# The first tile's two halves on two queues: sync engine and ScalarE, with the first two weights changed over

## The chip, the core and the metric

The kernel runs on one core of a Trainium2 chip. A core has TensorE (PE, matrix products), VectorE (DVE), ScalarE (ACT), GpSimd (POOL) and SyncE (SP). Transfers between the large memory (HBM) and the on-chip memory (SBUF) are put on queues by SP, ACT or GpSimd and moved by 16 DMA engines. TensorE writes into PSUM, from where VectorE and ScalarE take the results. The metric is the time of one execution in microseconds of device time.

## The reference

The input x has 2048 rows of 640. It is normalized over its rows (layer norm, no weights), and two branches use the result:

```python
xn = _layernorm(x, axis=-1)
s = _A_ref(xn, A_wqkv, A_wo)     # q, k, v = xn @ wqkv; 32 heads of 20; each position looks at
                                 # 8 earlier ones, 2 apart; softmax; then @ wo
g = _silu(_B_ref(xn, B_w1, B_w2))  # silu(silu(xn @ w1) @ w2), inner width 1536
return x + s * g
```

All inputs are float32. The output has to agree with a float32 computation.

## The kernel before

**Numbers in two parts.** Each operand of a product is split into a high part (a copy rounded to the faster format float32r) and a low part (the value less its high part). A product is the sum of three: high by high, low by high, high by low. In the names, `th` and `tl` are the two parts of the transposed normalized rows, `w` holds both parts of a weight. A high part is a ScalarE copy, a low part a subtraction on VectorE or GpSimd.

**Stages.** The 2048 rows are worked in four groups of 512 rows (`g`), each of four tiles of 128 rows (`t`). For each group there are four quarters of q, k and v (8 heads each, five weight chunks of 128 rows by 480 columns, a chunk being "a weight" in what follows), with attention on VectorE beside them; the output projection of the group before; and the two layers of the feed-forward branch. Weights pass through a ring of seven buffers. In the first pass they come as float32 and are split on the chip (`raw_load` starts the transfer; `w_load` does ScalarE's copy in line 371 and the subtraction in line 374); the split parts are stored and loaded again for later groups.

**The start.** `first_quarter` handles the first group's first quarter tile by tile. TensorE is kept running on 20 transposes of the identity (line 532) until the first tile is there. The tile comes in two halves of 320 columns, each a transfer of 128 rows of 1280 bytes (line 588 of the kernel before). `begin(t)` does a tile's statistics (line 544, one for each half), their aggregate (545), the square root on ScalarE (413), the reciprocal (415), and the normalization in two pieces of 384 and 256 columns (549). `turn(t)` transposes the tile on TensorE (558), copies the high half out (562) and makes the low half (566). `products` are the matrix products (579), three for each weight and tile: for the first tile, first those with the high part of each weight in turn, against `th` and `tl`; those with the low part follow after the second tile's transposes.

**The order.** Nothing in this kernel is ordered by hand on an engine. Every operation is handed to `Weave` with its engine, an estimated duration, what it reads and writes, and a priority (a small number goes first). `order()` lays out the whole kernel in a simulated time: again and again it takes, of all engines' next possible starts, the earliest, and among the operations of that engine that can start then, the one with the lowest priority number. TensorE's operations keep the order in which they were added. The result is the order in which each engine gets its instructions; on the chip an engine works in that order, and waits where the planner was too hopeful. For a transfer the planner adds up bytes at 310 KB/us over all queues, and adds 1.9 us for the landing:

```python
if o.nbytes:
    dma = max(dma, t + dur) + o.nbytes / self.RATE
    o.end = dma + self.LAND + (self.EARLY[1] if lanes[e][-1] and t < self.EARLY[0] else 0.0)
```

`EARLY` is a correction, in the first 10 us of the plan, for every transfer that is not the first on its queue. An operation with `lock` set isn't planned beside another one with it: these are the VectorE and GpSimd operations that read two inputs in SBUF. A HOP of 0.12 us is planned between engines. Operations with priorities of 140 or more give way to more urgent ones that can start up to 1 us later.

`BY_ACT` names the weights whose transfer ACT issues (by number in the order of the first pass), with priority -1; the others are issued by SP with priority 1 + k. `X_AT` holds the priorities of the second, third and fourth tiles' transfers, and a lower one than a weight's (or the same, as they were added earlier) puts the tile ahead of that weight on SP's queue. With the values of the kernel before, SP issues: both halves of the first tile, weight 1 (the second), the second tile, weights 2 to 5, the third tile, weight 6, the fourth tile, weights 7 to 9. ACT issues weight 0 alone.

The halo memset (line 641) sets the two top rows of each quarter's k and v buffer to zero. It belongs to GpSimd, which also does the subtractions of weights 0, 1 and 5 to 9 in the first group.

Of the kernel before, what the change touches and what calls it, by code (L numbers as in the profile page):

```python
# [8 lines left out]
F32 = mybir.dt.float32  # L9
F32R = mybir.dt.float32r  # L10
AF = mybir.ActivationFunctionType
OP = mybir.AluOpType
AX = mybir.AxisListType

P = 128
S, D, F, H, DH = 2048, 640, 1536, 32, 20
W = 8
DC, FC = D // P, F // P
# [12 lines left out]
WARM, WARM2 = 20, 3  # L31
HOLD = 3.4
LO = 10
BY_ACT = (0,)
QAT = 48
X_AT = 3, 7, 8
TILE_AT = 1, 1.5, 5, 6
LOW_AT = 3
NOW = 1
# [19 lines left out]
class Weave:  # L59
# [8 lines left out]
    LANES = 8  # L68
    RATE = 310e3
    LAND = 1.9  # L70
    EARLY = 10.0, 0.2
    TABLE = 1.28
    PATIENCE = 1.0

# [98 lines left out]
def local_attention_silu_ffn(ctx: ExitStack, tc: tile.TileContext, x, wqkv, wo, w1, w2, out):  # L173
    nc = tc.nc
# [6 lines left out]
    add = wv.add  # L181

    xg = x.rearrange("b (g p j) d -> (b g) p j d", p=P, j=J)
# [4 lines left out]
    def rows(view, g):  # L188
        h, par = groups[g]
        return view[h, :, par::2, :]  # L190
# [25 lines left out]
    XIN = sb.tile([P, T, D], F32, name="xin")  # L216
# [27 lines left out]
    po = lambda n: 0.11 + n * 0.0023  # L244
# [4 lines left out]
    def act(n, fn, reads, writes, prio, table=None):  # L249
        add("ACT", ac(n), fn, reads, writes, prio, table=table)  # L250
# [5 lines left out]
    def dma(fn, reads, writes, nbytes, prio, dur=0.45):  # L256
        add("SP", dur, fn, reads, writes, prio, nbytes=nbytes)
# [41 lines left out]
    for u in units:  # L299
        n = seen[u] = seen.get(u, 0) + 1  # L300
# [13 lines left out]
    def raw_load(k):  # L314
# [24 lines left out]
        else:  # L339
            m = wo if u[0] == "wo" else w2  # L340
            src, dst = m[u[1] * P:(u[1] + 1) * P, :], r
        if k in BY_ACT:
            add("ACT", 0.65, lambda: nc.scalar.dma_start(dst, src), [], kr, -1, nbytes=n * P * 4)
# [4 lines left out]
    def w_load():  # L348
        i = loaded[0]
        if i >= len(units):  # L350
            return
        loaded[0] += 1
        u, s = units[i], i % RING
        n = width(u)
        r = WR[s]
        at = start(u)
        both = r.rearrange("p (s d) -> p s d", s=2)[:, :, at:at + n]
        whi, wlo = both[:, 0], both[:, 1]
        kh, kl = ("wh", s), ("wl", s)
        due = clock[0]  # L360
        if what[i] == "load":
            src = halves[u]
            add("POOL", 1.0, lambda: nc.gpsimd.dma_start(both, src), [("half", u)], [kh, kl], due + 10,  # L363
                nbytes=2 * n * P * 4)
            return
        k = fresh.index(i)
        if not k:
            raw_load(0)
            rawn[0] = 1
        raw, kr = raws.pop(i)  # L370
        act(n, lambda: nc.scalar.activation(whi, raw, AF.Copy), kr if k else kr + [("sd", 0)], [kh], 1000 + due)
        pool_does = k < LO and k not in ON_DVE
        eng, cost, by = ("POOL", po(n), nc.gpsimd) if pool_does else ("DVE", dv(n), nc.vector)
        add(eng, cost, lambda: by.tensor_tensor(
            out=wlo, in0=raw, in1=whi.bitcast(F32), op=OP.subtract), [kh] + kr, [kl],
            due if pool_does else LOW_AT if k < LO else 50, lock=True)
        if what[i] == "store":
            kept = dram.tile([P, 2, n], F32, name="half_" + "_".join(map(str, u)))
            halves[u] = kept
            dma(lambda: nc.sync.dma_start(kept, both.bitcast(F32)), [kh, kl], [("half", u)], 2 * n * P * 4,  # L380
                due + 25)
        while rawn[0] <= (min(k + 6, early - 1) if k < early - 2 else k + 2):
            raw_load(rawn[0])
            rawn[0] += 1
# [141 lines left out]
    def first_quarter(i):  # L526

        ps, ws = {}, []

        def warm(n, where):  # L530
            for k in range(n):
                nc.tensor.transpose(where[:, tsl(k % T)], ident, ident)
        pe(4.5, lambda: warm(WARM, ROT[0]), ["consts"], [("rot", 0)])

        PARTS = (0, 3), (3, DC)

        def begin(t):

            at = TILE_AT[t]
            st, ks = ST[t % 2], ("st", t % 2)  # L540
            for k in range(2):
                cs = slice(k * 320, (k + 1) * 320)
                kx = ("xin", t) if t or k else ("xin", t, "a")
                dve(320, lambda k=k, cs=cs: nc.vector.bn_stats(out=st[:, k, :], in_=XIN[:, t, cs]), [kx], [ks + (k,)], at)  # L544
            dve(60, lambda: nc.vector.bn_aggr(out=MV[:, t, :], in_=st), [ks + (0,), ks + (1,)], [("mv", t)], at)
            ln_rstd(t, t + 1, at)
            for j, (a, b) in enumerate(PARTS):
                cs = slice(a * P, b * P)
                dve((b - a) * 64, lambda cs=cs: nc.vector.tensor_scalar(  # L549
                    out=XIN[:, t, cs], in0=XIN[:, t, cs], scalar1=MV[:, t, 0:1], scalar2=SD[:, 1, t:t + 1],  # L550
                    op0=OP.subtract, op1=OP.mult), [("rs", t), ("mv", t), ("xin", t)], [("xn", t, j)], at, lock=True)

        def turn(t):
            parts = [p + (j,) + rot() for j, p in enumerate(PARTS)]
            for a, b, j, tp, kp in parts:
                def go(a=a, b=b, tp=tp):
                    for c in range(a, b):
                        nc.tensor.transpose(tp[:, tsl(c - a)], XIN[:, t, c * P:(c + 1) * P], ident)  # L558
                pe(0.11 * (b - a), go, [("xin", t), ("xn", t, j)], [kp])
            for a, b, j, tp, kp in parts:  # L560
                v = tp[:, :(b - a) * P].rearrange("p (c n) -> p c n", n=P)
                act((b - a) * P, lambda a=a, b=b, v=v: nc.scalar.activation(TH[i][:, a:b, tsl(t)], v, AF.Copy),  # L562
                    [kp], t_keys(i, range(a, b), [t], ["th"]), 0)
            for a, b, j, tp, kp in parts:
                v = tp[:, :(b - a) * P].rearrange("p (c n) -> p c n", n=P)
                dve((b - a) * P, lambda a=a, b=b, v=v: nc.vector.tensor_tensor(
                    out=TL[i][:, a:b, tsl(t)], in0=v, in1=TH[i][:, a:b, tsl(t)].bitcast(F32), op=OP.subtract),
                    [kp] + t_keys(i, range(a, b), [t], ["th"]), t_keys(i, range(a, b), [t], ["tl"]), 0)

        def products(t, steps):  # L570

            o, kp = ps[t]
            for k, c in steps:
                x, kx = (TL, "tl") if k == 1 else (TH, "th")
                wh, wl, kh, kl = ws[c]
                w, kw = (wl, kl) if k == 2 else (wh, kh)
                first, last = t not in given, given.get(t, 0) == 3 * DC - 1
                given[t] = given.get(t, 0) + 1
                pe(mm(480), lambda x=x, c=c, w=w, first=first, last=last: nc.tensor.matmul(  # L579
                    o[:, :3 * CQ], x[i][:, c, tsl(t)], w, start=first, stop=last), [(kx, i, c, t), kw], [kp])  # L580

        def passes(*ks):
            return [(k, c) for k in ks for c in range(DC)]

        given = {}
        for k in range(2):
            cs = slice(k * 320, (k + 1) * 320)
            dma(lambda cs=cs: nc.sync.dma_start(XIN[:, 0, cs], rows(xg, 0)[:, 0, cs]), [],
                [("xin", 0) if k else ("xin", 0, "a")], P * 320 * 4, 0)
        for k, p in enumerate(X_AT):  # L590
            load_x(0, k + 1, prio=p)
        begin(0)
        for k in range(RING):
            w_load()
        for t in range(1, T):
            begin(t)
        for c in range(DC):
            ws.append(w_next("q", 0, c))
        for t in range(T):
            b, kp = bank()  # L600
            ps[t] = b, kp
        turn(0)
        pe(0.11 * WARM2, lambda: warm(WARM2, ACC[5]), [], [("acc", 5)])
        products(0, [(k, c) for c in range(DC) for k in (0, 1)])
        turn(1)
        products(0, [(2, c) for c in range(NOW)])
        products(1, passes(0, 1))
        products(0, [(2, c) for c in range(NOW, DC)])
        turn(2)
        products(1, passes(2))  # L610
        products(2, passes(0, 1))
        turn(3)
        products(2, passes(2))
        products(3, passes(0, 1, 2))
        wv.writer["first"] = wv.ops[-1]
        w_done(DC)
        return ps

    def qkv_phase(g, i, io):
        for q in range(NQ):  # L620
            if g == 0 and q == 0:
                ps = first_quarter(i)
            else:
                ps = [bank() for t in range(T)]
                for c in range(DC):
                    wh, wl, kh, kl = w_next("q", q, c)
# [12 lines left out]
                        o_chunk(g - 1, O_AT[q, c], io)  # L639
            if g == 0:  # L640
                add("POOL", 2.0, lambda q=q: nc.gpsimd.memset(KV[q][0:2, :, 0:HALO, :], 0.0), ["first"] if q else [],
                    [("halo", q, 1, 0), ("halo", q, 2, 0), ("halo", q, 3, 0), ("halo", q, 4, 0)], 1 + q)
            for t in range(T):
                evac_qkv(g, q, t, *ps[t])
            halo(g, q)
# [221 lines left out]
```

## Time and profile before

| | before |
|---|---|
| runs (us) | 641.28, 643.10, 642.76; median 642.76 |
| profiled execution (us) | 641.45, span 639.6 |
| TensorE products | 632.7 us, 99% of the span, 3495 instructions |
| weight loads of TensorE | 572.5 us, 90% |
| VectorE | 538.7 us, 84% |
| ScalarE | 207.2 us, 32% |
| GpSimd | 123.4 us, 19% |
| mean granted TensorE clock | 0.999 |
| chain that ended last | PE 98%, DVE 1%, DMA 1% |
| read from and written to HBM | 109.55 MB, 34.16 MB |

The profile is of one execution. Its span goes from the first to the last instruction and is 1.8 us shorter than the time of the same execution. Times within the profile count from the span's start. The mark "q" behind an engine's name means its sequencer, which issues transfers; a row of the timeline or of the chain gives the start, the length, the engine, the line, and for the timeline the output and input. A row of stretches gives, after the length, the busy time of PE, of PE's weight loads, of DVE, ACT and POOL, each with the number of instructions, then the granted clock, the share of the DMA engines in use and GB/s. A row of a queue gives its packets, the megabytes, and the share of the 16 DMA engines' time.

### The profile page before, as it was taken

Reading aid. Unit: us, or ns where it says so; the run is one execution under the profiler, and the core shown is the slowest. Engines: PE = TensorE matmul, PEld = TensorE weight load, DVE = VectorE, ACT = ScalarE, POOL = GpSimd, SP = SyncE. Lnnn points to the kernel's source line nnn. Section 1 sums busy time; section 2 is a strip of 40 time slices with the busy share of each in tenths; the row PEclk is TensorE's granted clock in tenths of the full one; section 3 lists DMA queues with packets and bytes.
Section 4 is the critical chain, followed back from the end, with each engine's and each line's share of the span. In section 5 each row is a group of like instructions: output and inputs, shape, how many; then the busy total and the mean of one; then the engine's idle time right before and its main releaser. Section 6 shows DMA issues by size and latency. Waiting matters only on the chain.

```text
span 639.6 us, 9015 instructions
## 1 busy us (share of the span) xinstructions
PE 632.7 (99%) x3495; PEld 572.5 (90%) x3495; DVE 538.7 (84%) x539; ACT 207.2 (32%) x401; POOL 123.4 (19%) x168
## 2 busy tenths in 40 slices
PE   7999999999999999999999999999999999999997
PEld 6888889999889989999888999999988899899997
DVE  6699999999999989999839998999106999899814
ACT  4436453443534022324332112223313222233230
POOL 4500000001101241111222125111222213411100
PEclk9999999999999999999999999999999999999999
DMA  9999999777999998657699978865679995885522
GB/s 280 338 306 318 335 403 378 293 233 225 282 328 323 291 303 256 194 167 214 183 267 276 291 219 272 304 186 165 170 208 258 285 301 194 270 305 185 186 83 82
DMA packets 74154, 162.44 MB, mean 254 GB/s; under 512 B 5648, under 2 KB 47088, under 8 KB 74112
## 3 DMA queue, kind: packets, MB, share of 16 engines
q0 software_dynamic: 26672, 82.58, 44.9%
q1 hardware_dynamic: 47040, 79.05, 39.7%
q8 instruction: 27, 0.44, 0.3%
q10 hardware_dynamic: 400, 0.25, 0.1%
q14 instruction: 15, 0.12, 0.1%
HBM read 109.55 MB, written 34.16 MB: 225 GB/s over the span
## 4 chain that ended last, share of the span: by engine, by line
PE 98%; DVE 1%; DMA 1%; ACT 0%; issue 0%; SPq 0%
PE acc L667 22%; PE acc L669 15%; PE acc L633 10%; PE acc L634 10%; PE acc L635 10%; PE rot L788 9%; PE rot L786 9%; PE rot L787 9%; PE rot L429 2%; PE acc L579 2%; DMA xin<-in_A_x_dram 1%; PE rot L756 0%; DVE xin L549 0%; PE rot L558 0%; DVE st L544 0%; ACT th L562 0%
## 5 line engine op out<-in xcount | busy, mean ns | idle before, releaser
L633 PE MATMUL acc<-w,th 128*128 128x480 f32 x300 | 114.7, 382 | 0.0
L667 PE MATMUL acc<-w,sh 128*128 128x384 f32 x384 | 113.6, 335 | 0.0
L634 PE MATMUL acc<-w,tl 128*128 128x480 f32 x300 | 113.5, 378 | 0.0
L635 PE MATMUL acc<-w,th 128*128 128x480 f32 x300 | 113.4, 378 | 0.0
L669 PE MATMUL acc<-w,sh 128*128 128x256 f32 x384 | 107.1, 279 | 0.0
L477 DVE TENSOR_TENSOR pr<-q,kv 128x2560 f32<-128x2560 f32 x32 | 90.3, 2821 | 11.6 <-DMA kv<-kv 11.2
L786 PE MATMUL rot<-th,w 128*128 128x512 f32 x240 | 95.4, 398 | 0.0
L788 PE MATMUL rot<-th,w 128*128 128x512 f32 x240 | 94.0, 391 | 0.0
L787 PE MATMUL rot<-tl,w 128*128 128x512 f32 x240 | 93.9, 391 | 0.0
L509 DVE TENSOR_TENSOR pr<-e,kv 128x2560 f32<-128x2560 f32 x32 | 90.3, 2821 | 0.8
L480 DVE TENSOR_REDUCE l<-pr 128x128 f32<-128x2560 f32 x32 | 90.0, 2814 | 0.2
L363 POOL DMA_DIRECT2D w<-half_q x52 | 37.4, 719 | 233.3 <-DVE pr L514 93.5
L514 DVE TENSOR_TENSOR pr<-pr 128x1280 f32<-128x1280 f32 x64 | 76.6, 1197 | 1.1
L792 ACT ACTIVATE sh<-rot 128x512 fp32r<-128x512 f32 x48 | 28.8, 600 | 149.3 <-PE rot L788 146.6
L669 PEld LDWEIGHTS acc<-w,sh 128*128 128x128 f32 x384 | 72.3, 188 | 1.6
L667 PEld LDWEIGHTS acc<-w,sh 128*128 128x128 f32 x384 | 72.1, 188 | 1.7
L363 POOL DMA_DIRECT2D w<-half_w x72 | 38.6, 537 | 179.3 <-PE acc L669 96.4
L635 PEld LDWEIGHTS acc<-w,th 128*128 128x128 f32 x300 | 56.3, 188 | 8.5
L634 PEld LDWEIGHTS acc<-w,tl 128*128 128x128 f32 x300 | 56.4, 188 | 8.0
L633 PEld LDWEIGHTS acc<-w,th 128*128 128x128 f32 x300 | 56.3, 188 | 8.0
L667 PE MATMUL acc<-w,sl 128*128 128x384 f32 x192 | 57.8, 333 | 0.0
L434 DVE TENSOR_TENSOR tl<-rot,th 128x512 fp32r<-128x512 f32 x35 | 23.8, 681 | 38.3 <-ACT th L433 38.2
(88 smaller groups left out, 1002.9 us busy)
## 6 DMA issues: line engine op xcount, KB each, us to landing
w<-half_w POOLq DMA_DIRECT2D x72, 640.0 KB, 5.5
w<-half_q POOLq DMA_DIRECT2D x52, 480.0 KB, 5.1
half_w<-w SPq DMA_DIRECT2D x24, 640.0 KB
half_q<-w SPq DMA_DIRECT2D x20, 480.0 KB
w<-half_wo POOLq DMA_DIRECT2D x15, 640.0 KB, 5.4
kv<-kv SPq DMA_DIRECT2D x16, 560.0 KB
kv<-kv SPq DMA_DIRECT2D x16, 420.0 KB
gate<-in_B_w_dram SPq DMA_DIRECT2D x16, 320.0 KB
```

The costliest lines, as they stand in the source:

```text
L477: dve(2560, lambda t=t: nc.vector.tensor_tensor(out=PR, in0=win(qq[:, t:t + 2, :], W, 0), in1=win(kv[:, 0, t:t + 2, :], W, CQ), op=OP.mult ...
L480: dve(2560, lambda t=t: nc.vector.tensor_reduce(out=l[:, t:t + 2].rearrange("p t w h -> p (t w h)"), in_=PR.rearrange("p t w (h d) -> p (t ...
L509: dve(2560, lambda t=t, v=v: nc.vector.tensor_tensor(out=PR.rearrange("p t w (h d) -> p t (w h) d", d=DH), in0=e[:, t:t + 2].rearrange("p ...
L514: dve(2 * n * CQ, lambda n=n: nc.vector.tensor_tensor(out=PR[:, :, 0:n, :], in0=PR[:, :, 0:n, :], in1=PR[:, :, n:2 * n, :], op=OP.add), [] ...
L633: nc.tensor.matmul(o, hi, wh, start=c == 0, stop=False)
L634: nc.tensor.matmul(o, lo, wh, start=False, stop=False)
L635: nc.tensor.matmul(o, hi, wl, start=False, stop=c == DC - 1)
L667: nc.tensor.matmul(a[t][0][:, :CA], st, w[:, :CA], start=first, stop=last)
L669: nc.tensor.matmul(b[t // 2][0][:, h * CB:(h + 1) * CB], st, w[:, CA:], start=first and h == 0, stop=last, skip_group_check=True)
L786: nc.tensor.matmul(h, wh[:, cs], TH[i][:, c, :], start=c == 0, stop=False)
L787: nc.tensor.matmul(h, wh[:, cs], TL[i][:, c, :], start=False, stop=False)
L788: nc.tensor.matmul(h, wl[:, cs], TH[i][:, c, :], start=False, stop=c == DC - 1)
```

## The change

```diff
--- before.py
+++ after.py
@@ -31,9 +31,10 @@
 WARM, WARM2 = 20, 3
 HOLD = 3.4
 LO = 10
-BY_ACT = (0,)
+HALVES = 1
+BY_ACT = (1,)
 QAT = 48
-X_AT = 3, 7, 8
+X_AT = 3, 6, 8
 TILE_AT = 1, 1.5, 5, 6
 LOW_AT = 3
 NOW = 1
@@ -68,7 +69,7 @@
     LANES = 8
     RATE = 310e3
     LAND = 1.9
-    EARLY = 10.0, 0.2
+    EARLY = 10.0, -0.4
     TABLE = 1.28
     PATIENCE = 1.0
 
@@ -368,12 +369,15 @@
             raw_load(0)
             rawn[0] = 1
         raw, kr = raws.pop(i)
-        act(n, lambda: nc.scalar.activation(whi, raw, AF.Copy), kr if k else kr + [("sd", 0)], [kh], 1000 + due)
+        act(n, lambda: nc.scalar.activation(whi, raw, AF.Copy), kr + [("sd", 0)] * (k < 2), [kh], 1000 + due)
         pool_does = k < LO and k not in ON_DVE
         eng, cost, by = ("POOL", po(n), nc.gpsimd) if pool_does else ("DVE", dv(n), nc.vector)
-        add(eng, cost, lambda: by.tensor_tensor(
-            out=wlo, in0=raw, in1=whi.bitcast(F32), op=OP.subtract), [kh] + kr, [kl],
-            due if pool_does else LOW_AT if k < LO else 50, lock=True)
+        parts = HALVES if pool_does and k < DC else 1
+        for j in range(parts):
+            cs = slice(j * n // parts, (j + 1) * n // parts)
+            add(eng, po(n // parts) if pool_does else cost, lambda cs=cs: by.tensor_tensor(
+                out=wlo[:, cs], in0=raw[:, cs], in1=whi[:, cs].bitcast(F32), op=OP.subtract), [kh] + kr,
+                [kl if j == parts - 1 else kl + (j,)], due if pool_does else LOW_AT if k < LO else 50, lock=True)
         if what[i] == "store":
             kept = dram.tile([P, 2, n], F32, name="half_" + "_".join(map(str, u)))
             halves[u] = kept
@@ -585,8 +589,9 @@
         given = {}
         for k in range(2):
             cs = slice(k * 320, (k + 1) * 320)
-            dma(lambda cs=cs: nc.sync.dma_start(XIN[:, 0, cs], rows(xg, 0)[:, 0, cs]), [],
-                [("xin", 0) if k else ("xin", 0, "a")], P * 320 * 4, 0)
+            by = nc.scalar if k else nc.sync
+            add("ACT" if k else "SP", 0.4, lambda by=by, cs=cs: by.dma_start(XIN[:, 0, cs], rows(xg, 0)[:, 0, cs]), [],
+                [("xin", 0) if k else ("xin", 0, "a")], -2, nbytes=P * 320 * 4)
         for k, p in enumerate(X_AT):
             load_x(0, k + 1, prio=p)
         begin(0)
@@ -639,7 +644,7 @@
                         o_chunk(g - 1, O_AT[q, c], io)
             if g == 0:
                 add("POOL", 2.0, lambda q=q: nc.gpsimd.memset(KV[q][0:2, :, 0:HALO, :], 0.0), ["first"] if q else [],
-                    [("halo", q, 1, 0), ("halo", q, 2, 0), ("halo", q, 3, 0), ("halo", q, 4, 0)], 1 + q)
+                    [("halo", q, 1, 0), ("halo", q, 2, 0), ("halo", q, 3, 0), ("halo", q, 4, 0)], 1 + 12 * q)
             for t in range(T):
                 evac_qkv(g, q, t, *ps[t])
             halo(g, q)
```

In words, one by one:

- The first half of the first tile stays on SP's queue; the second half is issued by ACT. Both have priority -2 and so come ahead of everything else on their queues.
- `BY_ACT` is 1 instead of 0: ACT issues the second weight, behind the half, and SP the first weight, behind its half.
- The third tile's transfer has priority 6 instead of 7, which puts it one place earlier on SP's queue, ahead of weight 5.
- In the planner, early transfers that are not the first on their queue are taken to land 0.4 us before the general rule instead of 0.2 us after it.
- ScalarE's copies of both of the first two weights are held until the square root of the first tile; before, that was so for the first.
- The memsets of the second, third and fourth quarter's halo have the priorities 13, 25 and 37 instead of 2, 3 and 4.
- GpSimd's subtraction of a weight can be cut into `HALVES` parts; this is 1.

Lines behind these in the file move down by a few: what is line 588 before is 593 after, and so on.

## The prediction

> **What bounds the kernel now.** I read the page first, then the stretches of the span, then the chain that ended last at the start, and last the queues.
>
> ```profile
> span 639.6 us, 9015 instructions
> ...
> 1.50:6.00 4.50, 4.41 (x20) 4.01 (x20) 1.22 (x4) 1.74 (x4) 1.73 (x1) 1.00 0.85 261
> 6.00:24.00 18.00, 16.21 (x83) 13.40 (x84) 14.42 (x38) 10.68 (x27) 5.57 (x5) 1.00 1.08 354
> 24.00:60.00 36.00, 36.00 (x168) 31.29 (x167) 33.62 (x36) 16.31 (x36) 9.40 (x6) 1.00 1.07 313
> ...
> 600.00:630.00 30.00, 30.00 (x192) 28.77 (x192) 11.21 (x17) 6.84 (x13) 2.08 (x4) 1.00 0.29 90
> ```
>
> The first number after each stretch's length is TensorE's busy time. From 24 us on it is busy all the time (36.00 of 36.00, 30.00 of 30.00), so the middle has nothing to give, and whatever moves TensorE's stream at 24 us moves the end by the same amount. Between 6 and 24 us it is busy 16.21 of 18.00: 1.79 us are idle, and 0.09 us in the stretch before. The change adds and removes no TensorE work, so about 1.88 us is the most it can win. Where that idle time hangs, the chain of waits tells (start, length, what):
>
> ```profile
> 1.21 3.65 DMA xin<-in_A_x_dram
> ...
> 4.88 0.50 DVE st L544
> ...
> 5.41 0.22 DVE mv L545
> ...
> 5.65 0.30 ACT sd L413
> ...
> 5.98 0.17 DVE sd L415
> ...
> 6.18 1.69 DVE xin L549 x2
> 7.87 0.80 DVE st L544 x2
> 8.67 0.47 DVE tl L566
> ...
> 9.18 2.23 PE acc L579 x9
> ```
>
> The second half of the first tile is on its way until 4.86 us. Then come its statistic, the aggregate, the square root, the reciprocal, the normalization in two pieces, two statistics of the second tile, the low half of the first tile, and TensorE's products. The timeline has the issues:
>
> ```profile
> 0.75 0.63 ACTq L343 DMA_DIRECT2D pr<-in_A_wqkv_dram  x1
> 0.76 0.87 SPq L588 DMA_DIRECT2D xin<-in_A_x_dram  x2
> ...
> 1.38 4.53 PE L532 MATMUL rot<-ident 128*128 128x128 f32 x20 [1.38 <-POOL ident masks.py:199]
> 1.41 1.28 ACT L827 ACT_TABLE_LOAD   x1 [1.41 <-PEq L853]
> ...
> 1.67 0.68 SPq L345 DMA_DIRECT2D pr<-in_A_wqkv_dram  x1
> 2.39 0.60 SPq L400 DMA_DIRECT2D xin<-in_A_x_dram  x1
> ...
> 3.14 0.50 DVE L544 BATCH_NORM_STATS2 st<-xin 128x6 f32<-128x320 f32 x1 [1.70 <-DMA xin<-in_A_x_dram]
> ```
>
> Both halves leave SP back to back, but the first is used at 3.14 us and the second only at 4.88. What lay between them is in the queues (q1 is SP's, q10 ACT's). The lines are the busy share in 75 ns slices of 0 to 3 us, then the packets of 0 to 2.35, 0 to 2.75 and 0 to 3.05 us:
>
> ```profile
> DMA  0000000000000000000000031746569986844556
> ...
> q1 hardware_dynamic: 79, 0.10, 16.0%
> ...
> q1 hardware_dynamic: 143, 0.16, 20.1%
> q10 hardware_dynamic: 43, 0.03, 5.0%
> ...
> q1 hardware_dynamic: 144, 0.16, 18.1%
> q10 hardware_dynamic: 137, 0.09, 10.9%
> ```
>
> Data begins at 1.73 us (slice 23). 144 packets and 0.16 MB are one half: 128 rows and, I take it, 16 completion writes. So at 3.05 us SP's queue had delivered the first half and nothing of the second, while ACT's queue, silent until 2.35, had moved 0.09 MB of the first weight. The second half was overtaken by the weight. That is what the change turns round.
>
> **The change, part by part.**
>
> *The halves.* ACT's queue now issues the second half at 0.75 us and SP's the first. I let the second half take the place that the first weight had: first packet about 2.4 us. The first half took 1.73 to 2.75 us, 1.0 us, and VectorE had it 0.4 us later (3.14). So the second half is moved by 3.4 and used at 3.8 us, an estimate. The bounds: 3.14 if both halves flow at once, and 4.86 less the earlier issue (1.21 to 0.75), 4.40, if only the issue is saved.
>
> Not all of this counts. Before, only one statistic stood behind the landing; the other was done at 3.64. In the planner's order the second half is now expected first, since ACT's issue comes first in its sum of bytes: 0.40 + 0.53 + 1.90 = 2.83, against 3.36 for the first half. VectorE will wait for the second half and then do both statistics, 0.50 each: 3.80 to 4.80, and the aggregate starts at 4.82 instead of 5.41. The first term is **0.59 us** (bounds 1.25 and -0.01).
>
> *Square root to normalization* follows on one path and shifts along: the aggregate to the first piece takes 5.41 to 6.18, so that piece starts at 5.59. The second piece depends on GpSimd:
>
> ```profile
> 5.85 1.22 ACT L371 ACTIVATE w<-pr 128x480 fp32r<-128x480 f32 x2
> ...
> 6.53 2.41 POOL L374 TENSOR_TENSOR w<-pr,w 128x480 fp32r<-128x480 f32 x2 [3.30 <-ACT w L371]
> ...
> L549 DVE TENSOR_SCALAR xin<-xin,mv,sd 128x256 f32<-128x256 f32 x1 | 1.3, 1296 | 0.0
> ...
> L549 DVE TENSOR_SCALAR xin<-xin,mv,sd 128x256 f32<-128x256 f32 x1 | 0.4, 410 | 0.0
> ```
>
> The two lower lines are this piece in the first tile and in the second. With a weight's subtraction on GpSimd beside it, it took 1296 ns instead of 410. Does that stay? The queues, 0 to 4.1 and 0 to 5.5 us (total, whatever the queue):
>
> ```profile
> DMA packets 751, 0.62 MB, mean 150 GB/s; under 512 B 44, under 2 KB 751, under 8 KB 751
> ...
> DMA packets 1177, 1.04 MB, mean 190 GB/s; under 512 B 69, under 2 KB 1088, under 8 KB 1177
> ```
>
> The first tile and two weights are 0.33 + 2 x 0.25 = 0.82 MB, reached on the straight line between these rows at 4.8 us, used 0.4 later, at 5.2. The square root, moved up by 0.59, frees ACT at 5.3. So the casts (the second weight's first, by the planned order) begin about when the weights are there, GpSimd starts some 0.68 later as before, and the piece meets it again: 1.30 us, end at 7.28. The extra dependence of the second cast on the square root changes nothing, as both casts already follow it.
>
> *The second tile.* By the planner's sum (0.40 for the first issue, 0.53 for each half, 0.79 for each of two weights, 1.06 for itself, then 1.90 less 0.40) it lands at 5.60, and its statistics take 5.72 to 6.68. The low half of the first tile is planned to be ready at 6.39 (warm-up done at 5.32, transposes 0.33, ACT's copy 0.50, two hops of 0.12), so the second tile's statistics stay ahead of it on VectorE, which takes its work in order. So the real landing of the second tile is what is late next. Its 2560 B packets are those under 8 KB that are not under 2 KB; 0 to 6.7 and 0 to 6.85 us:
>
> ```profile
> DMA packets 1597, 1.37 MB, mean 205 GB/s; under 512 B 89, under 2 KB 1470, under 8 KB 1597
> ...
> DMA packets 1659, 1.41 MB, mean 206 GB/s; under 512 B 90, under 2 KB 1531, under 8 KB 1659
> ```
>
> 127 of 128, then all. With the same 0.4 us it is usable at 7.25, hardly ahead of my 7.28. It is issued third on SP's queue instead of fourth, one issue (0.5 us) earlier, with the same bytes ahead of it. So its bounds are 6.75 and 7.25, and with the chain's 7.87 they allow a gain of 1.12 and 0.62. I keep **0.59 us**: statistics at 7.28, low half at 8.08, products at 8.59 instead of 9.18. From there VectorE, ACT and TensorE repeat the old sequence. The second tile's transposes, at 11.4 in the old chain, have the same work ahead of them.
>
> *What is hidden.* ACT issues two transfers instead of one (0.63 for the weight, some 0.4 for the half), so its table load starts near 1.8 us and ends near 3.1; the square root needs it at 5.1. If that cover were gone it would cost 0.4. The memsets:
>
> ```profile
> 23.64 1.23 POOL L374 TENSOR_TENSOR w<-gate,w 128x480 fp32r<-128x480 f32 x1 [9.31 <-ACT w L371]
> 24.81 5.79 POOL L641 MEMSET kv<- 2x2240 f32 x3
> 30.57 2.83 POOL L374 TENSOR_TENSOR w<-gate,w 128x480 fp32r<-128x480 f32 x2
> ```
>
> With priorities 13, 25, 37 against about 20 for the two last subtractions (the planner's clock there: 4.5 of warm-up, 60 products of 0.2155 and the transposes), only the first memset stays ahead of them. They then end near 29.6 instead of 33.4. The 24 to 60 row shows no TensorE wait to remove, so this is nothing; the other way, the late memsets are through near 33.5 us, and the halo of the third quarter is written only after its products, near 50 us (two quarters of 60 products from 24 us, at 36.00 / 168 us each). HALVES = 1 gives one part, as before.
>
> *The sum.* 0.59 us off the profiled execution's 641.45 is 640.9. The three runs shown lie at 641.28, 642.76 and 643.10, their median 1.3 above the profiled one; off the median it gives **642.2**. A measurement of this kernel tells about 0.3%, 1.9 us, from no change.
>
> **The rivals.**
>
> *Only the issue is saved.* The second half lands at 4.40, two statistics follow, and the aggregate starts at 5.42: no gain, 642.8. Against it: the 137 weight packets ahead of any of the second half's, which the new order puts behind it. The Trainium skill, "DMA: Bandwidth & Descriptors", section "Issuing engines are not separate DMA queues", says just this: transfers from several engines run on the same 16 DMA engines and interleave, so a second issuer saves only issue time. By that rule the result is 642.8; the queue rows show that who issues also decided which transfer came first.
>
> *All of it comes.* Both halves land near 3.2, the weights after the normalization has passed (piece of 0.41 us), the second tile at 6.75: 1.12 us, 641.6. The ceiling of 1.88 us would give 640.9.
>
> *The second tile comes late.* Weights now lead on both queues, and the second tile must share with the second weight on ACT's queue and the third on its own. If it is used after 7.87 us, every microsecond more is one lost, with the low half and all products waiting behind the statistics on VectorE. If all of the third and fourth weights passed it (0.82 + 0.33 + 0.49 = 1.64 MB, beyond the 1.41 MB of 6.85 us by 0.23 MB, 0.65 us at 354 GB/s), it would be used at 7.9: no gain. If the fifth passed it too (0.25 MB, 0.7 us), at 8.6: a loss of 0.7, 643.5. For it: the planned landing moved 0.85 us earlier (6.45 to 5.60), which no row supports.
>
> *The change does not do what it says*: a half on ACT's queue starts no sooner than 3.05 us, as the second half did. It gives the first rival's time.
>
> **How the numbers follow.** The forecast has 0.55, saving only the issue (with the change being empty) 0.17, all of it 0.13, the late second tile 0.15. Their times, 641.6 to 643.5, all lie within 0.3% of 642.76; the runs' own scatter of 1.8 us, 0.9 to each side, decides the rest. The range takes the forecast's bounds and the late tile with most of that scatter: 640.4 to 644.0. Faster by over 0.3% needs 640.8 or less: part of "all of it" and a low median under the forecast, 0.17. Slower by over 0.3%, above 644.7, needs a late tile and a high median, or an order of the planner that I have not foreseen, 0.13. Within: 0.70.
>
> **What would show it.** On the changed profile's timeline: SP issues one L588, ACT one L588 and then a weight; the first statistic starts at 3.8 us and the second directly behind; the aggregate at 4.8; the second piece of L549 near 1.3 us; the second tile's statistics at 7.3 with little wait for a transfer; products from 8.6. Idle of TensorE in 6 to 24 us falls by about 0.6. I am wrong if the second half's packets still follow a weight's, if the second tile's statistics wait past 7.9 us, or if TensorE waits anywhere after 24 us.

## Result and profile after

| | before | after |
|---|---|---|
| runs (us), 17 each | 641.28 to 643.83, median 642.51 | 641.05 to 642.21, median 641.22 |
| ratio after to before | | 0.9983 (95% interval 0.9976 to 0.9989) |
| profiled execution (us) | 641.45, span 639.6 | 641.25, span 639.5 |
| mean granted TensorE clock, profiled | 0.999 | 1.0 |

The kernel is 1.1 us faster by the ratio (0.7 to 1.5 us), 1.3 us by the medians. But the two profiled executions differ by only 0.2 us, and the runs after lie close together (16 of 17 within 0.45 us) where those before spread over 2.5 us. The profile answers for the 0.2; the rest has to be looked for in what the profiled execution of before did not show.

First the chain of waits of the changed kernel (start, length, what). Line numbers are those of the changed file.

```profile
0.75 3.28 DMA xin<-in_A_x_dram
...
4.05 0.90 DVE st L548 x2
...
4.98 0.22 DVE mv L549
...
5.75 1.70 DVE xin L553 x2
7.45 0.80 DVE st L548 x2
8.24 0.47 DVE tl L570
...
8.75 2.22 PE acc L583 x9
...
11.86 0.89 DVE tl L570 x2
12.74 0.81 DVE st L548 x2
...
13.78 0.75 DVE st L548 x2
...
14.63 0.68 DVE xin L553
...
15.35 0.76 PE rot L562 x5
...
24.22 0.21 PE acc L638
```

The second half is used at 4.05 us instead of 4.88, both statistics follow it, and the products with the low half start at 8.75 instead of 9.18: 0.43 us earlier. At 24 us TensorE's next quarter starts at 24.22. In the kernel before the same chain has this, and between the two points no VectorE:

```profile
12.31 3.30 PE acc L579 x14
15.61 0.65 PE rot L558 x5
16.26 3.24 PE acc L579 x15
19.50 0.55 PE rot L558 x5
20.05 4.32 PE acc L579 x20
24.37 0.21 PE acc L633
```

So of 0.43 us, 0.26 are left at the third tile's transposes (15.35 against 15.61) and 0.15 at 24 us. In the changed kernel the chain runs over VectorE from 11.86 to 15.30: there TensorE waits 0.18 us for the third tile's normalization, which it had not done before. That normalization starts at 14.63 instead of 14.96, so only 0.33 us earlier, and its first piece takes longer (before, then after; the number behind the bar's comma is its time in ns):

```profile
L549 DVE TENSOR_SCALAR xin<-xin,mv,sd 128x384 f32<-128x384 f32 x1 | 0.5, 479 | 0.0
...
L553 DVE TENSOR_SCALAR xin<-xin,mv,sd 128x384 f32<-128x384 f32 x1 | 0.7, 664 | 0.0
```

In the changed kernel GpSimd does two subtractions of weights beside it (12.67 to 15.08 us); before, the last one was through at 14.34. In 6 to 24 us TensorE is busy 16.47 us, against 16.21, so its idle time there falls by 0.26 us and not by the 0.6 that were forecast.

The queues of the changed kernel, 0 to 2.75 and 0 to 3.6 us (q1 SP, q10 ACT; the last of the lines is the total, with the packets by size):

```profile
q1 hardware_dynamic: 77, 0.10, 23.9%
q10 hardware_dynamic: 37, 0.05, 4.6%
...
q1 hardware_dynamic: 144, 0.16, 23.4%
q10 hardware_dynamic: 319, 0.28, 22.3%
...
DMA packets 463, 0.44 MB, mean 122 GB/s; under 512 B 32, under 2 KB 463, under 8 KB 463
```

At 2.75 us SP's queue has moved 77 packets where it had moved 143 before, and ACT's 37. The halves flow beside each other and slow each other. By 3.6 us both are through: the 32 packets under 512 B are, by the prediction's count of 16 for one half, those that end the two of them. ACT's queue is into its weight by then.

### The profile page after: what moved, and what is told of

It is laid out like the page before. It is cut to its first block, busy times and chain, and to the rows that moved or that the text cites. A ratio compares the mean times of both kernels' runs of the same rounds, so it can differ in the third digit from the quotient of the medians.

```text
span 639.5 us, 9016 instructions
## 1 busy us (share of the span) xinstructions
PE 632.2 (99%) x3495; PEld 572.2 (89%) x3495; DVE 540.1 (84%) x539; ACT 204.1 (32%) x399; POOL 122.3 (19%) x168
## 4 chain that ended last, share of the span: by engine, by line
PE 97%; DVE 1%; DMA 1%; ACT 0%; issue 0%
PE acc L672 22%; PE acc L674 15%; PE acc L638 10%; PE acc L639 10%; PE acc L640 10%; PE rot L793 9%; PE rot L791 9%; PE rot L792 9%; PE rot L433 2%; PE acc L583 2%; DMA xin<-in_A_x_dram 1%; DVE st L548 1%; DVE xin L553 0%; PE rot L761 0%; PE rot L562 0%; DVE tl L570 0%
## 5 line engine op out<-in xcount | busy, mean ns | idle before, releaser
L518 DVE TENSOR_TENSOR pr<-pr 128x1280 f32<-128x1280 f32 x64 | 78.3, 1224 | 1.1
L793 PEld LDWEIGHTS rot<-th,w 128*128 128x128 f32 x240 | 45.0, 188 | 9.9
```

The costliest lines, as they stand in the source:

```text
L518: dve(2 * n * CQ, lambda n=n: nc.vector.tensor_tensor(out=PR[:, :, 0:n, :], in0=PR[:, :, 0:n, :], in1=PR[:, :, n:2 * n, :], op=OP.add), [] ...
L793: nc.tensor.matmul(h, wl[:, cs], TH[i][:, c, :], start=False, stop=c == DC - 1)
```

## Experiments: where the rest comes from

Two theories. **C, the clock**: in most executions of the kernel before, TensorE's granted clock is down for some microseconds at the start, which the profiled one happened not to show, and the change prevents it. (The clock records of that execution begin at 6.60 us with the full clock and keep it.) **L, the landing**: the earlier second half is worth the 1.1 us, and the profile shows too little of it.

**The kernel before, once more** (no edit).

> The kernel before, unchanged, to see what differs between its own executions. Theory C (clock): most of its executions have TensorE at a lower granted clock for a few microseconds at the start. Then the runs' mean clock is lower (0.996 to 0.998) in the runs near 642.5 us than in those near 641.4 us, where it is 0.999 or 1.0, and a profile of a slow one shows full clock only from some 8 to 12 us. Theory L (landing): the second half of the first tile lands at varying times; then clock and time are unrelated, and a slow profile shows the second statistic 1 us later than 4.88 us.

Measured: 642.24 us, ratio 0.9999 (0.9990 to 1.0007). This time the profiled execution took 642.26 us. Its stretches, the clock being the first number behind the last instruction count in brackets, some of TensorE's instructions, and two rows of its chain:

```profile
4.66:8.08 3.42, 1.73 (x13) 1.26 (x12) 2.99 (x7) 1.78 (x5) 1.89 (x2) 1.00 1.04 319
8.08:11.49 3.41, 3.41 (x11) 2.58 (x10) 3.37 (x10) 2.52 (x6) 1.33 (x2) 0.50 1.08 352
```

```profile
8.85 0.77 PE L579 MATMUL acc<-w,tl 128*128 128x480 f32 x1
9.41 0.60 PE L579 MATMUL acc<-w,th 128*128 128x480 f32 x1
9.81 0.60 PE L579 MATMUL acc<-w,tl 128*128 128x480 f32 x1
...
11.68 0.38 PE L579 MATMUL acc<-w,th 128*128 128x480 f32 x1
11.89 0.38 PE L579 MATMUL acc<-w,tl 128*128 128x480 f32 x1
```

```profile
4.55 0.51 DVE st L544
...
25.23 0.22 PE acc L633
```

The second statistic starts at 4.55 us instead of 4.88 and the products at 8.85 instead of 9.18, both earlier than in the first profile of this kernel, so no transfer is late. But from 8.08 to 11.49, a stretch of 3.41 us, the clock is at half and the products follow each other at 0.40 us instead of 0.21. The chain reaches the next quarter at 25.23 us instead of 24.37. By the trace's clock records full clock had been granted at 4.66 (what lies before the first record is written as 1.00 in the views), and in the 3.41 us up to 8.08 TensorE was busy for only 1.73. The expectation had the clock open late; here it opened early and then fell.

The same can be counted without a profile, since each run comes with its mean clock; half a clock for 3.41 us of 640 is a mean of 0.997. Of 92 executions of the kernel before in these experiments, 47 had 0.997 or less, with a median of 642.57 us and none below 642.16; the other 45 had a median of 641.63. The groups overlap: ten of the 45 took 642.0 us or more. Of the 17 of the changed kernel, one had it: 0.996, at 642.21 us. Theory C holds here, for about half of the executions; L's late statistic is not there.

**Longer warm-up in the kernel before.**

```diff
-WARM, WARM2 = 20, 3
+WARM, WARM2 = 23, 3
```

> The kernel before with 23 instead of 20 warm-up transposes, which the planner does not know of, so the order is the same; they fill TensorE's idle stretch from 5.9 to 6.6 us. Theory C: the clock opens in time in nearly all executions, so the runs gather near 641.4 us, a ratio of 0.998 to before. Theory L: no transfer moves, so nothing changes: ratio 1.000, and the runs scatter as before, 641.3 to 643.8 us.

Measured: 641.27 us (641.09 to 641.39), ratio 0.9987 (0.9978 to 0.9995). Three more transposes in an idle stretch, with no transfer moved, do what the whole change does. The lowest mean clock in its 11 runs is 0.999, as theory C expected.

**The same in the changed kernel, and both on one chip.**

> The changed kernel with 23 instead of 20 warm-up transposes, order unchanged. Theory C (clock): the one execution in 17 at 642.2 us goes, the rest stays: 641.1 to 641.5 us, median 641.2; set against the kernel before with 23 transposes it shows what the earlier landing alone is worth at the same clock. By the two profiles' streams at 24 us (24.22 and 24.37) that is 0.15 us; theory L (landing) asks for 1.1 us between these two.

> The kernel before with 23 warm-up transposes once more, on the same chip as the changed kernel with 23. Theory C: 641.3 us, within 0.3 us of it. Theory L: 642.3 us, 1.1 us above it.

Measured: 641.25 us (ratio 0.9982, 0.9973 to 0.9991) with the change, 641.38 us (0.9983, 0.9974 to 0.9992) without it. With the clock held up in both, the change is worth 0.13 us by the medians, which their intervals can't tell from nothing; the two profiles have the next quarter at 24.30 and 24.34 us. Theory L asked for 1.1.

**Shorter warm-up in the changed kernel.**

```diff
-WARM, WARM2 = 20, 3
+WARM, WARM2 = 14, 3
```

> The changed kernel with 14 warm-up transposes, order unchanged; all transfers as in the changed kernel, but TensorE has been idle for 1.4 us more before the first tile. Theory C: the clock falls back or opens late in most executions, so 642.5 us or more with a mean clock of 0.994 to 0.997, slower than the kernel before. Theory L: nothing changes, 641.2 us.

Measured: 642.68 us (641.64 to 643.24), ratio 1.0005 (0.9996 to 1.0014): the gain is gone with every transfer in its new place. That it would be slower than the kernel before isn't shown. Only 4 of 11 runs have a mean clock of 0.997 or less. The profiled one, at 642.02 us, has 1.0: there the matmul records show slow products before 10 us (0.60 us each, then 0.38), and its clock records begin only at 10.12. So the mean misses a clock that opens late, and counting by it is a lower bound. Late openings may be what the ten of the 45 with 642.0 us or more have; no profile is of one of them, so that isn't shown.

**The halves alone**: the halves on two queues, the first two weights changed over and the second cast held, with the third tile, the planner's correction and the memsets as before.

```diff
-BY_ACT = (0,)
+BY_ACT = (1,)
...
-... kr if k else kr + [("sd", 0)], [kh], 1000 + due)
+... kr + [("sd", 0)] * (k < 2), [kh], 1000 + due)
...
-            dma(lambda cs=cs: nc.sync.dma_start(XIN[:, 0, cs], rows(xg, 0)[:, 0, cs]), [],
-                [("xin", 0) if k else ("xin", 0, "a")], P * 320 * 4, 0)
+            by = nc.scalar if k else nc.sync
+            add("ACT" if k else "SP", 0.4, lambda by=by, cs=cs: by.dma_start(XIN[:, 0, cs], rows(xg, 0)[:, 0, cs]), [],
+                [("xin", 0) if k else ("xin", 0, "a")], -2, nbytes=P * 320 * 4)
```

> The kernel before with the halves on two queues and the first two weights changed over alone; third tile's place, planner's correction and memset priorities as before. In its order the low half of the first tile stands between the second tile's two statistics instead of behind both, so the first product with a low half should come about 0.4 us earlier than the changed kernel's 8.75 us. Theory L: it gives the whole gain or more, ratio 0.998 or below. Theory C: the gain depends on how TensorE's idle stretches fall, so also near 0.998, with its runs as close together as the changed kernel's (641.05 to 641.5 us but for one).

Measured: 641.40 us (640.90 to 641.86), ratio 0.9989 (0.9980 to 0.9998); no run below a mean clock of 0.999. The scatter, 0.96 us, is twice that of the changed kernel without its one execution at 642.21. The low half between the statistics did not bring the 0.4 us: the chain waits for the fourth weight instead.

```profile
3.40 5.61 DMA pr<-in_A_wqkv_dram
9.03 0.60 ACT w L371
9.82 0.60 ACT w L371
```

**The other parts alone**, first without and then with the hold of the second cast:

```diff
-X_AT = 3, 7, 8
+X_AT = 3, 6, 8
-    EARLY = 10.0, 0.2
+    EARLY = 10.0, -0.4
-... ("halo", q, 4, 0)], 1 + q)
+... ("halo", q, 4, 0)], 1 + 12 * q)
```

> The kernel before with only the other parts: third tile's priority 6, planner's correction -0.4, memset priorities. Theory L: no first half moves, ratio 1.000. Theory C: only an order that shortens TensorE's early idle time helps; the second tile's statistics come first as before, so also 1.000, with runs scattered from 641.3 to 643.8 us.

> The kernel before with the other parts (third tile's priority, planner's correction, memset priorities) and with the second cast held until the first square root, as in the changed kernel; halves and first two weights as before. If the 3 us lost without the hold came from that cast standing ahead of the square root alone, they are gone. Theory C (clock): the start's waits are those of the kernel before, so its scatter too, 641.3 to 643.2 us, median about 642.2, ratio 1.000. Theory L: 1.000 as well.

Measured: 645.22 us, ratio 1.0047 (1.0035 to 1.0060), and with the hold 643.20 us, 1.0014 (1.0005 to 1.0023). Both expectations fell. Without the hold, ScalarE's order has a weight's cast ahead of each of the first two square roots, and each waits for its transfer:

```profile
5.38 0.60 ACT L371 ACTIVATE w<-pr 128x480 fp32r<-128x480 f32 x1 [2.46 <-DMA pr<-in_A_wqkv_dram]
5.89 0.28 ACT L413 ACTIVATE sd<-mv,epst 128x1 f32<-128x1 f32 x1
6.08 0.59 ACT L371 ACTIVATE w<-pr 128x480 fp32r<-128x480 f32 x1
7.38 0.60 ACT L371 ACTIVATE w<-pr 128x480 fp32r<-128x480 f32 x1 [0.71 <-DMA pr<-in_A_wqkv_dram]
7.89 0.28 ACT L413 ACTIVATE sd<-mv,epst 128x1 f32<-128x1 f32 x1
```

TensorE is idle longer, and the clock is at half until 14.8 us. With the hold that is gone, but the planner's new order costs about 0.6 us more by itself: the runs at full mean clock lie at 641.97 to 642.79 us and those with the clock down at 643.17 and above, where the medians of the kernel before are 641.63 and 642.57. So these parts cost time without the new transfers; which of the three does it was not tried.

**GpSimd held until the normalization is through**, on the changed kernel with 23 transposes:

```diff
...
-                out=wlo[:, cs], in0=raw[:, cs], in1=whi[:, cs].bitcast(F32), op=OP.subtract), [kh] + kr,
+                out=wlo[:, cs], in0=raw[:, cs], in1=whi[:, cs].bitcast(F32), op=OP.subtract), [kh] + kr + ["held"] * (k < 2),
...
+        add("POOL", 0.12, lambda: nc.gpsimd.tensor_tensor(out=HOLDT, in0=XIN[:, 0, D - 4:], in1=XIN[:, 0, D - 4:], op=OP.add),
+            [("xn", 0, 1)], ["held"], -1)
```

> The changed kernel with 23 warm-up transposes, and GpSimd's subtractions of the first two weights held until the first tile's normalization is through (a four-column sum on GpSimd that reads the normalized tile stands ahead of them). The second piece of the normalization should take 0.41 instead of 1.30 us and end near 6.6 us. If the second tile's landing is the next limit, at 7.25 us as the prediction had it, its statistics wait for it and start near 7.25: products 0.15 us earlier. If it lands by 6.8 us, which its packets in the changed kernel's queue (all begun by 6.4 us) suggest, products come 0.5 us earlier, at 8.2 us, and up to that much comes off the time unless a later step takes it back, as it took back 0.28 of the first 0.43 us.

Measured: 641.10 us (640.91 to 641.82), ratio 0.9984 (0.9975 to 0.9992), the lowest median of all, 0.15 below the changed kernel with 23 on the same chip. The intervals don't separate the two, and by the ratios (0.9984 against 0.9982) it is no faster. What it shows is the next limit:

```profile
L554 DVE TENSOR_SCALAR xin<-xin,mv,sd 128x256 f32<-128x256 f32 x1 | 0.4, 406 | 0.0
...
6.75 0.89 DVE L549 BATCH_NORM_STATS2 st<-xin 128x6 f32<-128x320 f32 x2 [0.35 <-DMA xin<-in_A_x_dram]
...
8.14 0.49 PE L584 MATMUL acc<-w,tl 128*128 128x480 f32 x1 [0.41 <-DVE tl L571]
```

The piece takes 406 instead of 1304 ns with GpSimd out of its way, the second tile is there at 6.7 us, and the products start at 8.14, 0.61 us earlier than in the changed kernel. The next quarter starts at 24.03 instead of 24.22: 0.19 of the 0.61 us are left. VectorE again takes most of it back ahead of the third tile.

**The fifth weight's subtraction on GpSimd**, on top of that:

```diff
-ON_DVE = (2, 3, 4)
+ON_DVE = (2, 3)
```

> The changed kernel with 23 transposes and the hold, and the fifth weight's subtraction on GpSimd instead of VectorE, so that VectorE reaches the third tile's statistics before the second tile's low half. If VectorE's work ahead of the third tile's normalization is what took the earlier start back, the third tile's transposes wait no more, TensorE's stream at 24 us is up to 0.4 us earlier than with the hold alone (24.03), and the median is near 640.8 us. If GpSimd's work beside it stretches VectorE's, nothing or less: 641.1 us or above.

Measured: 643.04 us, ratio 1.0020 (1.0011 to 1.0029), slower than the kernel before, and by a way that neither half of the expectation named. The planner, given more room on VectorE, put the third tile's statistics and a low half in between the two pieces of the second tile's normalization, and TensorE waits in the middle of its transposes:

```profile
10.56 0.49 PE L563 MATMUL rot<-ident,xin 128*128 128x128 f32 x3
12.54 0.44 PE L563 MATMUL rot<-ident,xin 128*128 128x128 f32 x2 [1.49 <-DVE xin L554]
```

## Why the prediction was right, and where it was wrong

The range held the time, and the direction was right; the gain was forecast at 0.59 us and is 1.1. It came by another way than the prediction's: at the same clock the forecast chain is worth about 0.1 us. That the time lies in the range is therefore luck in good part. The range is 3.6 us wide and holds the time of the kernel before as well; the forecast of 642.2 is 1.0 us from the 641.22 that were measured.

*What bounds the kernel.* This is the step that failed. The prediction took the one profiled execution for the kernel and the 1.3 us between it and the median for scatter. Most of that scatter was the clock, and it could be won: three transposes more take the median of the kernel before from 642.17 to 641.27 us. The ceiling of 1.88 us was no ceiling for the same reason: products at half clock count as busy (3.41 of 3.41 us from 8.08 to 11.49).

*The halves.* Used at 4.05 instead of 3.8 us, and the aggregate at 4.98 instead of 4.82. The estimate let the first half run alone and the second take the weight's slot; in fact both run side by side, and the second is moved by 3.6 us instead of 3.4. The two statistics in a row took 0.90 us instead of 1.00. The first term is 0.43 by these two profiles, not 0.59. Other profiles show how far one execution can be trusted for it: in the kernel before, with 20 or 23 transposes, the second statistic starts at 4.55 to 4.88 us and the aggregate at 5.08 to 5.41, in the changed one at 4.05 and 4.11, and at 4.98 and 5.03. So the term lies between 0.05 and 0.43. The rival by which only the issue is saved (landing 4.40, issue 0.46 earlier) fell by the packets: 37 of the second half by 2.75 us, where before none had come by 3.05, and no profile of the changed kernel uses it later than 4.11.

*Square root to normalization.* As forecast: the piece beside GpSimd takes 1.30 us, and the stretch from aggregate to statistics is the old one, shifted.

*The second tile.* Its statistics didn't wait for it, as forecast; the changed kernel's own profile shows no more than that it was there by 7.45 us. With GpSimd held, where the statistics do wait, they start at 6.75 us, the early bound given; with the fifth weight moved as well, at 7.09, nearer the late one (7.25). The rival in which it comes late did not come about.

*"From there VectorE, ACT and TensorE repeat the old sequence."* Wrong: only 0.15 of 0.43 us reached 24 us, since the planner set the work of VectorE and GpSimd anew and the third tile's normalization, 0.33 us earlier and with a piece of 664 instead of 479 ns, became the last to end.

*What is hidden.* The table load stayed hidden (1.86 to 3.14 us, square root at 5.22). The memsets did not move in the order:

```profile
23.49 1.23 POOL L378 TENSOR_TENSOR w<-gate,w 128x480 fp32r<-128x480 f32 x1 [8.41 <-ACT w L372]
24.66 5.79 POOL L646 MEMSET kv<- 2x2240 f32 x3
30.43 2.82 POOL L378 TENSOR_TENSOR w<-gate,w 128x480 fp32r<-128x480 f32 x2
```

All three are still ahead of the last two subtractions. The forecast compared priorities; the planner does so only among operations that can start at the same time, which is read from its rule and was not tried. It cost nothing either way: from 24 us on TensorE is busy all the time.

How the change keeps the clock up: the profile of the changed kernel had its clock opened at 4.67 us, nearly the same as the execution of before that lost it, and in the 3.41 us from there TensorE was busy 1.82 us instead of 1.73:

```profile
4.67:8.08 3.41, 1.82 (x15) 1.35 (x13) 2.98 (x7) 1.88 (x5) 1.99 (x2) 1.00 1.03 319
8.08:11.49 3.41, 3.15 (x18) 2.48 (x16) 3.37 (x10) 2.11 (x6) 0.43 (x1) 1.00 1.08 342
```

It kept the full clock. That so little decides is borne out by all twelve traces of these experiments. Divided into stretches of 3.41 us from the first clock record on, they show the full clock fall after every stretch in which TensorE was busy 1.73 us or less (0.81 in the run of the other parts without the hold), and stay after every stretch with 1.77 or more (1.77 at the end of the run with 14 transposes, 1.82 here and in the kernel before with 23, second run). That the earlier normalization gives the 0.1 us in most executions of the changed kernel remains an inference; shown is that filling the idle time alone (23 transposes) has the same effect and emptying it (14) undoes it. The Trainium skill, "TensorE: Matmul & The Clock Gate", section "What's actually happening", describes a free-running activity window of 3413 ns, with the full clock after a busy window and half after an idle one. The traces agree on the length (3.41 us), and on a phase that differs between executions: full clock was first recorded at 6.60 and 4.66 us in the two profiles of the kernel before, at 7.18 with 23 transposes, and at 4.67 in the changed kernel. They differ on the fall: a window that was half busy (1.73 of 3.41) was enough.

## What to carry to other kernels

Before a gain is sized, look at the spread of the runs: if the profiled one lies at its edge, profile again until a slower execution is caught, and set the two beside each other; here the second profile of the same kernel had most of the answer. A stretch of idle TensorE at the start can cost twice, once as waiting and again when the clock falls, so filling it with dummy work can be worth more than shortening it (here 0.9 us against about 0.1). An earlier landing in front of an in-order engine whose order is planned anew is worth only what the last engine in the chain lets through, and has to be followed to the point from which TensorE is never idle.

## What was not expected of the hardware

Twenty transposes of the identity, and nothing else, opened the full clock by 4.67 us in the profile of the changed kernel; in the first profile of the kernel before it came at 6.60. By the same stretches of 3.41 us as above, the clock opened after those in which the profile counts TensorE busy for 2.72 us or more, and not after those with 2.70 or less, so in these traces it took a larger share to open the clock than to keep it. Two transfers of 164 KB issued at the same moment on two queues share the engines as soon as the second has packets, from about 2.1 us, and the first took longer than with a queue beside it that was silent until 2.35 us (77 packets by 2.75 us instead of 143); the pair is still there sooner (used at 4.05 us instead of 4.88) than when a weight of 246 KB is let in between.
